# Dealing out weight conversions, and starting each group's first output tile one step sooner, in a fused gated-linear-attention and SoLU kernel

## The chip, the cores and the metric

The kernel runs on one core of one Trainium2 chip. The metric is the device time of one execution in microseconds, lower is better. A core has five engines, each with a queue of its own that it works through in order: TensorE (PE in the profile; its weight loads are shown apart as PEld), VectorE (DVE), ScalarE (ACT), GpSimd (POOL) and SyncE (SP), which here only issues transfers. Engines wait for each other by semaphores. TensorE writes to PSUM, which has eight banks.

## The reference

Two blocks are joined. The first is a gated linear recurrence over 768 tokens for 4 batches and 8 heads of width 48; the second multiplies by weights, applies a softmax-weighted activation and a layer norm, and multiplies by weights again (1024 hidden units).

```
for t in range(S):
    state = alpha[:, :, t, :, None] * state + einsum('bhd,bhe->bhde', k[:, :, t], v[:, :, t])
    y[:, :, t] = einsum('bhd,bhde->bhe', q[:, :, t], state)
x = y.transpose(0, 2, 1, 3).reshape(B * S, H * D)      # 3072 x 384
h = x @ w_in                                           # 3072 x 1024
e = exp(h - max(h));  solu = h * e / (sum(e) + 1e-9)
ln = (solu - mean(solu)) / sqrt(var(solu) + 1e-6) * g_ln
out = ln @ w_out                                       # 3072 x 384
```

q, k, v and alpha are float32. The three weight arrays come as float64 and have to be converted on the chip.

## The kernel before

The sequence is cut into six groups of 128 tokens per batch, 512 tokens in all. For every group the kernel computes attention (in a chunked form with scans for the decay), then the up product, the activation, and the down product. The whole order is written by hand: a manual schedule, in which the order of the code is the order on every engine's queue.

**The up part of a group.** `up(g, s)` runs for s = 0 to 7, one step for each 128 of the 1024 hidden units. TensorE makes h in PSUM (L394, one of two banks), ScalarE takes its exponential e (L408), VectorE makes u = h * e into `room` (L409), ScalarE squares u (L412). In the squares and exponentials lie the row sums for the norm, added up in `running` by POOL (e) and VectorE (u2) at L427. The norm is applied behind the down product as one factor for each row: `token_sums` (L454) gathers the sums on TensorE and VectorE once a group, and `finish` (L518) makes the factor on VectorE (L532 to L537) and POOL (a power, L546), scales on ScalarE (L548) and writes out.

**The down part.** A group has four tiles of 128 tokens (one for each batch), and the down product of a tile is eight matmuls, done in two halves of four (`down(n, half)`, L501). The tile's result lies in one of two PSUM banks until `finish` has read it. The halves of group g-1's four tiles are spread over the eight steps of group g, one in each step: `todo` (L909, L946) is the list of them. Group 0's downs stand in the prologue; so group 1 has none to do in its steps, and the last group's eight stand behind the loop.

**The attention of the next group.** Between the steps of group g the kernel does the attention of group g+1. Two plans, `usual` and `first` (L835 to L849), say at which step which piece is done, and whether at the head of the step, behind its up, in the middle or at its tail. `apart` (L243) and `keys_back` (L300) run on ScalarE, `queries` (L250) and `decay` (L255) on POOL, `scan_on`, `scan_back`, `masked` and the transposes on VectorE, `scores`, `read_state`, `read_values` and `next_state` on TensorE. `read_values` copies the result y to x on ScalarE (L363), which the next group's up reads. `scores` writes four banks (a0 to a3) that `keys_back`, the query transposes, y and others use in turn.

**The prologue.** The weights are fetched as eight pieces into slots of `room` (`fetch`, L567): pieces 0 to 3 are w_in, 4 to 7 are w_out. `bits(i)` (L603) converts a piece in five VectorE steps (L612, L615, L620, L623, L624). `in_range(i)` (L590) checks a piece in two ScalarE passes (L598, L601). `scaled(i)` multiplies a piece of w_out by the norm's gains (L631). Later pieces are fetched into slots whose earlier piece has been converted and checked. The eight steps of group 0 (L735) hold the conversions of pieces 2 to 5, two or three VectorE steps in each; pieces 6 and 7 are converted behind the loop (L759, L767). `alpha_over(g)` (L192) checks alpha in two ScalarE passes (L196); `load(alpha, an, g + 1)` may overwrite `an` only when it and `alpha_T(g)` (VectorE's transposes of alpha) have read it. `mean` (L638) sums w_out by column on TensorE, and `centre` (L655) adds the result to w_out on POOL in group 1, so that from group 1 on the mean of the norm needs no work of its own.

The loop of group 0 and the lines behind it, before the change:

```
    for f in range(FC):
        up_mm(0, f)
        if f == 4:
            array_sums(0, 0)
        up_act(0, f, (lambda: in_range(2 + f // 2, (f % 2,))) if f < 6 else None)
        bits(2 + f // 2, f % 2)
        ...
    bits(6)
    ...
    down(0, 0)
    scaled(6)
    bits(7)
    token_sums(0)
    alpha_T(1)
    down(1, 0)
```

Of the kernel before, what the change touches and what calls it, by code (L numbers as in the profile page):

```python
# [11 lines left out]
U32 = mybir.dt.uint32  # L12
I32 = mybir.dt.int32
AF = mybir.ActivationFunctionType
ALU = mybir.AluOpType
# [17 lines left out]
def fast_path(ctx, tc, q, k, v, alpha, moe_w_in, moe_w_out, moe_g_ln, out):  # L33
# [13 lines left out]
    B, H, S, D = q.shape  # L47
    NTOK, DM = out.shape
    DFF = moe_w_in.shape[1]
    G = S // P  # L50
# [136 lines left out]
    def alpha_T(g):  # L187
        nc.gpsimd.memset(aT[:, :, 0:1], 0.0)
        firsts(an, aT[:, 0:H, 1:SW])
        lasts(an, aT[:, H:NB, 1:SW])  # L190

    def alpha_over(g):  # L192
        x = an.rearrange("p h u d -> p (h u d)")
        sq = one.tile([P, 768], FP, name="sq").bitcast(U8)[:, 0 : x.shape[1]]
        for i, sign in enumerate((1.0, -1.0)):
            nc.scalar.activation(  # L196
                out=sq, in_=x, func=AF.Relu, scale=sign, bias=mone, accum_out=over[:, g, i : i + 1]
            )
# [201 lines left out]
    def up_act(g, f, between=None):  # L400
        d = gr[g]
        h = d["h"]
        if g:
            e, u2 = (ring.tile([P, T4], FP, name=x) for x in ("e", "u2"))
        else:
            e, u2 = (sT[:, f % 4, 4 * i : 4 * i + 4].rearrange("p b t -> p (b t)") for i in range(2))
        u = u_of(g, f)
        nc.scalar.activation(out=e, in_=h, func=AF.Exp)  # L408
        nc.vector.tensor_tensor(out=u, in0=h, in1=e, op=ALU.mult)  # L409
        if between:  # L410
            between()
        nc.scalar.activation(out=u2, in_=u, func=AF.Square)  # L412
        d[f] = e, u2
# [87 lines left out]
    def down(n, half, part=range(HF)):  # L501
        g, b = divmod(n, B)
        d = st[n]
        if half == 0 and 0 in part:
            d["o"] = ps_o.tile([P, 512], FP, tag="o", name="o")
        for f in (half * HF + i for i in part):
            nc.tensor.matmul(  # L507
                d["o"][:, 0 : DM + 1], lhsT=u_of(g, f)[:, b * P : b * P + P], rhs=w_out[:, f], start=(f == 0),
                stop=(f == FC - 1), skip_group_check=True,
            )  # L510
# [50 lines left out]
    def place(i):  # L561
        kind, f = pieces[i]
        return w_out[:, f : f + 2, 0:DM] if kind else w_in[:, :, f * P : f * P + 2 * P]
# [26 lines left out]
    def in_range(i, parts=(0, 1)):  # L590


        if not float64:
            return
        if 0 in parts:
            hi = raws[i][:, :, :, 1].bitcast(FP)
            squares[i] = one.tile([P, F], FP, name="sq").rearrange("p (c f) -> p c f", c=hi.shape[1])
            nc.scalar.activation(out=squares[i], in_=hi, func=AF.Square, accum_out=far[:, i, 0:1])  # L598
        if 1 in parts:
            sq = squares.pop(i)  # L600
            nc.scalar.activation(out=sq, in_=sq, func=AF.Exp, scale=-(2.0**24), accum_out=far[:, i, 1:2])  # L601

    def bits(i, part=None):  # L603
        if not float64:
            return
        lo, hi = raws[i][:, :, :, 0], raws[i][:, :, :, 1]
        if part != 1:
            made[i] = [
                lots[2 * (i % 2) + x].rearrange("p (c f) -> p c f", c=hi.shape[1]) for x in range(2)
            ]  # L610
            top = made[i][0].bitcast(U32)
            nc.vector.tensor_scalar(  # L612
                out=top, in0=hi, scalar1=3, scalar2=0x3FFFFFF8, op0=ALU.logical_shift_left, op1=ALU.bitwise_and
            )
            nc.vector.scalar_tensor_tensor(  # L615
                out=top, in0=hi, scalar=0xC0000000, in1=top, op0=ALU.bitwise_and, op1=ALU.bitwise_or
            )
        if part != 0:
            top, low = made.pop(i)
            nc.vector.tensor_scalar(  # L620
                out=low.bitcast(U32), in0=top.bitcast(U32), scalar1=0xFF800000, scalar2=None, op0=ALU.bitwise_and
            )
            nc.vector.scalar_tensor_tensor(out=low, in0=lo, scalar=2.0**-52, in1=low, op0=ALU.mult, op1=ALU.mult)  # L623
            nc.vector.tensor_tensor(out=place(i), in0=low, in1=top, op=ALU.add)  # L624

    def scaled(i):
# [103 lines left out]
    keys_back(0)  # L730
    in_range(0)
    bits(1)
    in_range(1)

    for f in range(FC):  # L735
        up_mm(0, f)
        if f == 4:
            array_sums(0, 0)
        up_act(0, f, (lambda: in_range(2 + f // 2, (f % 2,))) if f < 6 else None)

        bits(2 + f // 2, f % 2)
        if f == 0:
            next_state(0)
            fetch(4, 3)
            load_first(k, kn, 1)
            load_first(q, qn, 1)
            load(alpha, an, 1)
        elif f == 2:
            ends_k = ends_of(kn, "e")
        elif f == 3:  # L750
            fetch(5, 1)
            fetch(6, 2)
            ends_q = ends_of(qn, "u2")
        elif f == 5:
            fetch(7, 3)
            load_v(1)
        elif f == 6:
            scaled(4)
    bits(6)  # L759
    tk = three("tp_k", [(ps_a, "a2"), (ps_a, "a3"), (ps_h, "h")])  # L760
    turned(kn, ends_k, tk)
    load(k, kn, 2)
# [1 line left out]
    scaled(5)  # L764
    down(0, 0)
    scaled(6)
    bits(7)  # L767
    token_sums(0)
    alpha_T(1)
    down(1, 0)  # L770
    scaled(7)
    tq = three("tp_q", [(ps_a, "a0"), (ps_a, "a1")])
# [8 lines left out]
    mean(1)  # L781
    down(0, 1, (2, 3))
    hold(0)
    alpha_over(1)
    load(alpha, an, 2)
    tq += three("tp_q2", [(ps_h, "h")])
    turned(qn, ends_q, tq, range(H, NB))
    down(1, 1)
# [121 lines left out]
    for g in range(1, G + 1):  # L910
        rise, att = g < G, g + 1 < G
        plan = first if g == 1 else usual

        def at(where, s):
            for what in plan[where].get(s, "").split() if att else ():
                attend(g + 1, what)

        after = 3 if g == 1 else None
        if not rise:
            break  # L920
        for s in range(FC):
            at("head", s)
            if rise:
                up(g, s)
            if after is not None:
                finish(after)
                after = None
            if s == 0 and g < 3:
                next_state(g)
            if s == 0 and g > 1:  # L930
                token_sums(g - 1)
            at("behind", s)
            for f in centres.get(s, ()) if g == 1 else ():
                centre(f)
            if rise and s:
                running(g, s)
            at("middle", s)
            if todo:
                n, half = todo.pop(0)
                down(n, half)  # L940
                if half:
                    after = n
            at("tail", s)
        if after is not None:
            finish(after)
        todo = [(n, half) for n in range(g * B, g * B + B) for half in range(2)]  # L946


    for n, half in todo[:2]:
        down(n, half)  # L950
        if half == 0:
            token_sums(G - 1)
            last_norm()
    finish(G * B - B)
# [485 lines left out]
```

## Time and profile before

| what | value |
|---|---|
| time, median of 3 runs | 373.24 us (372.33 to 374.39) |
| the profiled execution's own time | 374.51 us |
| its span, first to last instruction | 372.6 us |
| mean granted TensorE clock | 0.995 |
| busy: TensorE / VectorE / ScalarE / POOL | 361.1 / 244.9 / 147.2 / 124.6 us |
| down products (L507), up products (L394) on TensorE | 134.8, 132.2 us busy |
| VectorE, the 40 conversion steps (L612, L615, L620, L623, L624) | 5.4 + 7.7 + 4.4 + 7.7 + 7.6 = 32.8 us busy |
| transfers | 36.06 MB, mean 97 GB/s |

How to read it: the profile shows one execution on the chip. A line names the kernel's line, the engine, the operation, and the tiles written and read; "[0.60 <-ACT x L363]" says that the engine stood idle for 0.60 us before the instruction and what ended that. TensorE's ends are modelled, so its busy time is no measure of how well it runs, but its idle time is idle. In a float32 product each matmul appears twice. A busy share is an average over stages with different limits; the stages here are the prologue (to about 100 us), the middle groups, and the last group with its tail.

### The profile page before, as it was taken

To read this page: it belongs to the slowest core of one execution; us is meant where nothing else is said; L and a number is where in the kernel's file an instruction comes from. 1 tells how busy PE (TensorE), PEld (TensorE's weight loads), DVE (VectorE), ACT (ScalarE), POOL (GpSimd) and SP (SyncE) were. 2 spreads that over 40 slices of the span, in tenths; PEclk is the share of its full clock that TensorE was granted. 3 is DMA by queue.
4 is the path that set the end of the run, shared out by engine and by line. 5 is a ranking of instruction groups with operands and counts; after the bars stand their busy time and mean duration, and the time that the engine had idled before them with its cause. 6 is when DMAs were issued, how large, how long until landed. Compare 5 with 4: busy or idle time off the path is not lost. (4 is left out here: it accounts for less than half of the span.)

```text
span 372.6 us, 10040 instructions
## 1 busy us (share of the span) xinstructions
PE 361.1 (97%) x4341; PEld 215.8 (58%) x4341; DVE 244.9 (66%) x375; ACT 147.2 (40%) x260; POOL 124.6 (33%) x129
## 2 busy tenths in 40 slices
PE   8889999979999999999999999999999999999994
PEld 7775355556755566566575566575555565555552
DVE  1997979978998888945666945666946223544500
ACT  3649853591556262251532251532231231332100
POOL 7020000001367973573114573114582211333200
PEclk9999999998999999999999999999999999999999
DMA  9995986066177608453036253004050000000011
GB/s 181 187 326 144 217 270 139 2 135 152 67 161 165 153 3 168 111 137 84 25 86 145 68 136 86 25 4 106 21 129 9 23 23 0 24 22 21 30 39 49
DMA packets 72871, 36.06 MB, mean 97 GB/s; under 512 B 48232, under 2 KB 70000, under 8 KB 72816
## 3 DMA queue, kind: packets, MB, share of 16 engines
q1 hardware_dynamic: 71792, 34.39, 39.5%
q10 hardware_dynamic: 1024, 0.92, 0.7%
q8 instruction: 36, 0.59, 0.7%
q14 instruction: 19, 0.16, 0.1%
HBM read 25.30 MB, written 4.72 MB: 81 GB/s over the span
## 5 line engine op out<-in xcount | busy, mean ns | idle before, releaser
L507 PE MATMUL o<-w_out,room 128*128 128x385 f32 x384 | 134.8, 495 | 0.0
L394 PE MATMUL h<-x,w_in 128*128 128x512 f32 x288 | 132.2, 599 | 0.6 <-ACT x L363 0.6
L507 PEld LDWEIGHTS o<-w_out,room 128*128 128x128 f32 x384 | 71.6, 191 | 55.3 <-issue 14.7
L394 PEld LDWEIGHTS h<-x,w_in 128*128 128x128 f32 x288 | 52.7, 189 | 58.3 <-issue 48.4
L409 DVE TENSOR_TENSOR room<-h,e 128x512 f32<-128x512 f32 x40 | 27.6, 690 | 60.0 <-ACT e L408 60.0
L408 ACT ACTIVATE e<-h 128x512 f32<-128x512 f32 x40 | 23.9, 597 | 93.8 <-PE h L394 93.6
L427 POOL TENSOR_TENSOR p<-p,e 128x512 f32<-128x512 f32 x30 | 42.5, 1416 | 27.3 <-ACT e L408 27.0
L412 ACT ACTIVATE u<-room 128x512 f32<-128x512 f32 x40 | 25.2, 630 | 38.2 <-DVE room L409 38.2
L546 POOL TENSOR_TENSOR r<-sums,mhalf 128x1 f32<-128x1 f32 x20 | 12.8, 639 | 77.3 <-DVE sums L537 77.1
L289 DVE TENSOR_TENSOR sT<-a,mask 128x512 f32<-128x512 f32 x43 | 26.7, 683 | 14.4 <-PE a L278 14.4
L427 DVE TENSOR_TENSOR p<-p,u 128x512 f32<-128x512 f32 x30 | 24.4, 814 | 7.2 <-ACT u L412 7.2
L204 DVE TENSOR_TENSOR_SCAN hT<-aT,unit 128x516 f32<-128x516 f32 x18 | 23.4, 1342 | 7.6 <-ACT aT L697 7.5
L204 DVE TENSOR_TENSOR_SCAN aT<-aT,seed 128x516 f32<-128x516 f32 x18 | 27.9, 1578 | 0.2
L278 PEld LDWEIGHTS a<-qv,kT 32*128 32x128 f32 x704 | 21.9, 189 | 8.8 <-DVE qv L799 2.7
L278 PE MATMUL a<-qv,kT 32*128 32x128 f32 x704 | 24.6, 282 | 2.1 <-DVE qv L799 1.9
L333 PE MATMUL y<-sT,vn 128*32 128x128 f32 x768 | 22.9, 274 | 1.0 <-issue 0.8
L212 POOL COPY fend<-hT 128x12 f32<-128x12 f32 x6 | 4.1, 676 | 59.0 <-DVE hT L204 59.0
L333 PEld LDWEIGHTS y<-sT,vn 128*32 128x32 f32 x768 | 20.8, 110 | 4.4 <-issue 3.8
L225 POOL TENSOR_TENSOR kT<-kT,hT 128x1024 f32<-128x1024 f32 (+1 forms) x8 | 14.2, 1805 | 21.1 <-DVE kT L179 21.1
L196 ACT ACTIVATE sq<-an,mone 128x1536 uint8<-128x1536 f32 x12 | 18.9, 1575 | 0.2
L548 ACT ACTIVATE o_sb<-o,r 128x384 f32<-128x384 f32 x16 | 9.3, 581 | 24.1 <-POOL r L546 24.1
L363 ACT COPY x<-y 128x384 f32<-128x384 f32 x24 | 11.2, 479 | 7.3 <-PE y L333 7.1
(148 smaller groups left out, 364.5 us busy)
## 6 DMA issues: line engine op xcount, KB each, us to landing
vn<-in_v_dram SPq DMA_DIRECT2D x24, 192.0 KB, 4.4
an<-in_alpha_dram SPq DMA_DIRECT2D x20, 192.0 KB, 4.2
out_dram<-o_sb SPq DMA_DIRECT2D x20, 192.0 KB, 1.9
room<-in_moe_w_out_dram SPq DMA_DIRECT2D x8, 384.0 KB, 4.8
kn<-in_k_dram SPq DMA_DIRECT2D x16, 192.0 KB, 4.2
qn<-in_q_dram SPq DMA_DIRECT2D x16, 192.0 KB, 3.9
lot<-qe SPq DMA_DIRECT2D x40, 64.5 KB, 2.1
lot<-qv SPq DMA_DIRECT2D x20, 129.0 KB, 2.4
```

What stands on the lines that cost most here:

```text
L196: nc.scalar.activation(out=sq, in_=x, func=AF.Relu, scale=sign, bias=mone, accum_out=over[:, g, i : i + 1])
L204: nc.vector.tensor_tensor_scan(out=o, data0=a, data1=s, initial=1.0, op0=ALU.mult, op1=ALU.add)
L225: nc.gpsimd.tensor_tensor(out=kT[:, part], in0=kT[:, part], in1=hk[:, part], op=ALU.mult)
L278: nc.tensor.matmul(a[b][:, i], lhsT=kT[quarter(b), kb], rhs=qv[quarter(b), qb, 0:P], start=not last and not i, stop=bool(last), tile_posit ...
L289: nc.vector.tensor_tensor(out=sT[:, b, half * NP : half * NP + NP], in0=a[b], in1=mask[:, None, :].to_broadcast([P, NP, P]), op=ALU.mult,)
L333: nc.tensor.matmul(y_bank(b)[quarter(r), a], lhsT=lhsT, rhs=rhs, start=(b, r) not in begun, stop=stop, tile_position=(row, 32 * r), skip_g ...
L394: nc.tensor.matmul(h, lhsT=w_in[:, a, f * P : (f + 1) * P], rhs=d["x"][:, a].rearrange("p b t -> p (b t)"), start=(a == 0), stop=(a == KC ...
L408: nc.scalar.activation(out=e, in_=h, func=AF.Exp)
L409: nc.vector.tensor_tensor(out=u, in0=h, in1=e, op=ALU.mult)
L412: nc.scalar.activation(out=u2, in_=u, func=AF.Square)
L427: eng.tensor_tensor(out=p, in0=d[0][i] if f == 1 else p, in1=d[f][i], op=ALU.add)
L507: nc.tensor.matmul(d["o"][:, 0 : DM + 1], lhsT=u_of(g, f)[:, b * P : b * P + P], rhs=w_out[:, f], start=(f == 0), stop=(f == FC - 1), skip ...
```

## The change

Four things are moved; no instruction is added or taken away.

1. The five steps of a conversion can be called one by one (`bit(i, k)`), and the 30 steps of pieces 2 to 7 are dealt out over the eight steps of group 0: 4, 2, 3, 3, 3, 3, 3 and 9 behind the u of each step, where 2 and 3 stood in turn and ten more behind the loop.
2. The check of piece 1 moves from ahead of group 0's loop into its step 4, and both halves of piece 4's check stand in step 5.
3. `alpha_over(1)` moves from behind `hold(0)` to where `bits(7)` stood, ahead of `token_sums(0)`, and `load(alpha, an, 2)` to just behind `alpha_T(1)`.
4. In groups 1 to 4 the first half of the group's own first tile is done in step 7 of that group, so that each of the later halves stands one step sooner and each `finish` at an odd step where it stood at an even one. Group 1, which had none, has one half in step 7; group 5 has none there, and in the tail its row sums stand behind both halves of its first tile, where they stood behind one.

```
-    in_range(1)
+    steps = [(i, step) for i in range(2, 8) for step in range(5)]
+    checks = {0: [(2, 0)], 1: [(2, 1)], 2: [(3, 0)], 3: [(3, 1)], 4: [(1, 0), (1, 1)], 5: [(4, 0), (4, 1)]}
+    def check(f):
+        for i, part in checks.get(f, ()):
+            in_range(i, (part,))
     for f in range(FC):
         up_mm(0, f)
...
-        up_act(0, f, (lambda: in_range(2 + f // 2, (f % 2,))) if f < 6 else None)
-        bits(2 + f // 2, f % 2)
+        up_act(0, f, lambda: check(f))
+        for _ in range((4, 2, 3, 3, 3, 3, 3, 9)[f]):
+            step = steps.pop(0)
+            if float64:
+                bit(*step)
...
-    bits(6)
...
     scaled(6)
-    bits(7)
+    alpha_over(1)
     token_sums(0)
     alpha_T(1)
+    load(alpha, an, 2)
     down(1, 0)
...
     hold(0)
-    alpha_over(1)
-    load(alpha, an, 2)
...
             at("middle", s)
+            if s == FC - 1 and g < G - 1:
+                todo.append((g * B, 0))
             if todo:
                 n, half = todo.pop(0)
                 down(n, half)
...
-        todo = [(n, half) for n in range(g * B, g * B + B) for half in range(2)]
+        todo = [(n, half) for n in range(g * B, g * B + B) for half in range(2)][g < G - 1 :]
     for n, half in todo[:2]:
         down(n, half)
-        if half == 0:
+        if half == 1:
             token_sums(G - 1)
             last_norm()
```

`bit(i, k)` holds the same five VectorE instructions that `bits` held, k choosing one of them.

## The prediction

> **What bounds the kernel now.** I read the busy tenths first. In the page's second part a slice is 9.3 us.
>
> ```profile
> PE   8889999979999999999999999999999999999994
> ...
> PEclk9999999998999999999999999999999999999999
> ```
>
> TensorE is full nearly everywhere, at full clock, except in slice 9 (74 to 84 us), where a clock digit falls too. So only what TensorE waits for can be won. Its waits, longest first:
>
> ```profile
> PE a L278 <- DVE qv L799: 1.9, 2, 1.4
> ...
> PE h L394 <- ACT x L363: 0.6, 1, 0.6
> PE sums L645 <- DVE cols L467: 0.6, 1, 0.6
> ```
>
> The other entries lie before 28 us, where nothing changes. The windows around the longest wait (columns: stretch, length, TensorE busy, granted clock, DMA):
>
> ```profile
> 79.00:79.77 0.77, 0.23 (x1) 1.00 1.11 224
> 79.77:81.60 1.83, 0.48 (x2) 1.00 0.76 140
> 81.60:82.95 1.35, 1.31 (x44) 1.00 0.46 107
> 82.95:86.36 3.41, 3.41 (x30) 0.50 0.55 122
> 86.36:90.00 3.64, 3.64 (x70) 1.00 0.92 213
> ```
>
> TensorE stands nearly idle for 2 us, and 1.3 us later its clock is halved for 3.41 us, which therefore hold only 1.7 us of full-speed work. The wait with its price is thus about 2.2 + 1.7 us. Who is late is in the timeline of VectorE:
>
> ```profile
> 34.27 0.69 DVE L409 TENSOR_TENSOR room<-h,sT 128x512 f32<-128x512 f32 x1 [1.88 <-ACT sT L408]
> ...
> 48.87 0.69 DVE L409 TENSOR_TENSOR room<-h,sT 128x512 f32<-128x512 f32 x1 [1.22 <-ACT sT L408]
> ...
> 54.81 0.69 DVE L409 TENSOR_TENSOR room<-h,sT 128x512 f32<-128x512 f32 x1 [0.74 <-ACT sT L408]
> ...
> 80.89 0.69 DVE L799 TENSOR_TENSOR qv<-tp_q,aT 128x512 f32<-128x512 f32 x1
> 83.91 0.69 DVE L289 TENSOR_TENSOR sT<-a,mask 128x512 f32<-128x512 f32 x1 [2.33 <-PE a L278]
> ```
>
> From 54.81 to 81.58 VectorE works without a gap: 13 conversion steps (to 66.05), row sums, alpha's transposes, six scans, keys, queries. Before that it idles 1.88 + 1.22 + 0.74 us, waiting for ScalarE's exponentials. The fault is order, not load. From 144 us on TensorE has no wait over 0.25 us.
>
> **Conversions dealt out.** A piece costs 0.55 + 0.96 + 0.55 + 0.96 + 0.96 us, with gaps 4.1. Before, 17 of 30 steps precede the last u (L409, 54.81) and 13 follow; after, 21 and 9. Does it fit? The first exponential ran at 33.66 because the check of piece 1 (31.72 to 33.66) stood before it; that check goes to step 4, so u starts at about 32.4, when the second conversion ends. From 32.4 to 54.81 are 22.4 us; 21 steps (17.1) and seven u's of 0.61 (4.3) are 21.4. Adding row by row, each u waiting for its exponential, I get the last u at 54.95, 0.14 late. The four steps that are gone from behind it ran from 55.41 to 58.47: 3.06 us. Net: the chain to the last qv is 2.9 us shorter, and that qv is ready at 78.7.
>
> The check moved into step 4 takes 1.9 us of ScalarE where it idled 1.33 us; piece 4's whole check then sits in step 5, and the exponential of step 6 starts about 0.3 us later (51.1 for 50.81); its u waited for VectorE until 51.93, which hides it. Transfers: piece 5 can be fetched from 42.8 (step 3 of piece 3 ends at 42.3, SP is busy until 42.82) and is needed at 49.6; the room loads took 3.5 to 8.6 us to land, median 5.2. So between 0 and 1.8 us of VectorE time; I take 0, by the median. Piece 7 goes out near 49.7 and is needed at 59.
>
> **Alpha's check and load sooner.** Two ScalarE passes with their reads, 71.94 to 75.36: 3.4 us. They now stand between the scalings of pieces 6 and 7. Piece 6 is converted at about 59.1, scaled by 60.5; the check ends at 63.9; the last conversion ends at 63.1, so the last scaling is 0.8 us late and done at 65.0. Behind it on ScalarE waits the mean's copy; TensorE comes to the mean's sums only at 65.8. Cost nothing; without that cover up to 0.8. The four loads of alpha leave SP at 67 and not from 75.34 to 77.13. SP issued the query moves behind them at 77.92; those now need qe at 75.0, and SP is free. Value nothing by itself: VectorE took alpha at 86.31 after the masks, not after the load.
>
> **What TensorE gains.** The 0.6 at the mean's sums goes, but the next wait swallows it: TensorE comes to the first scores of group 1 at about 78.4 and waits until 78.75, where it started at 81.64. That is 2.9. The remaining idle stretch is under 0.5 us, so I take the halved clock as gone: 1.7 more, with ends 0 and 1.7. At the second half of the scores TensorE is 4.6 sooner. VectorE is not: between the two masks stands alpha's transposition, now from 83.0 to 86.0, so the second mask, which began at 90.13, begins at about 85.95: 4.2. From there VectorE hardly stops, and POOL's queries and TensorE hang on it:
>
> ```profile
> 117.72 1.45 PEld L278 LDWEIGHTS a<-qv,kT 32*128 32x128 f32 x46 [0.88 <-POOL qv L253]
> ```
>
> So at the next scores 4.2 us remain, 0.4 given back.
>
> The Trainium skill, "TensorE: Matmul & The Clock Gate", section "HAM oscillation — how this bites in real kernels", says that idle gaps up to about 3.4 us leave the clock up. By that rule the halving has another cause and would remain, and the sum below would be 1.7 us less. This trace halves it after gaps of 0.54 and 1.38 us; I go by the trace.
>
> **Downs one step sooner.** The halves of a group stay eight; no work goes. At the end of group 1 TensorE waits for the copy of the last y:
>
> ```profile
> 136.95 2.84 PE L394 MATMUL h<-x,w_in 128*128 128x512 f32 x6 [0.60 <-ACT x L363]
> ```
>
> Now a down half of 2.6 us stands there: gain 0.6. It needs w_out's first four chunks centred by POOL; the fourth is done at 130.64 against 136.3. If POOL were late by more than 5.7 us the cover would be gone.
>
> The finishes move from even to odd steps, and this is the risk. At step 3 of groups 2 to 4 ScalarE must now scale a row block before it splits the queries (L245) and copies the keys (L305, L310). The scale waits for POOL's power (0.55), which now stands behind the queries' products and a running sum:
>
> ```profile
> 160.88 1.72 POOL L427 TENSOR_TENSOR p<-p,e 128x512 f32<-128x512 f32 x1
> ```
>
> and in ScalarE's timeline there are
>
> ```profile
> 160.08 1.32 ACT L245 ACTIVATE qv<-qe,parity 128x512 f32<-128x512 f32 x2
> 161.31 1.05 ACT L305 COPY kg<-tp 128x512 f32<-128x512 f32 x2
> 162.25 0.66 ACT L310 COPY kg<-tp 128x256 f32<-128x256 f32 x2
> ```
>
> Sum for group 2: 162.60 + 0.55 + 0.05 + 0.58 = 163.8; queries and keys, 2.82 from first to last, end at 166.6. TensorE's scores began at 166.62 and need the banks that the keys leave. Step 4's exponential waits behind them too, 2.4 us later than its 164.13; its bank is wanted only two steps on. The margin is nil, and in group 3 (running sum done at 218.53, scores at 222.53) the same; group 4 has no keys to copy. Bounds 0 to 0.5 each (POOL's running sums took between 1.27 and 1.79); I take 0.1 each, as the sums meet almost exactly. At step 5 the state's decay on POOL goes behind a power, from 167.9 to about 173.4, and is read at 178.75: nothing. At step 7 the scale comes ahead of the copies of y, up to 0.9 late; the next h follows down and state products 4 us later: nothing.
>
> **Last group.** The row sums stay as far behind the last h as before (two down halves). The power then has two whole halves, 5.2 us, before a bank is wanted; it and the first finish took from 348.9 to 352.9. Nothing.
>
> **The sum.** 4.2 + 0.6 - 0.2 = 4.6 us, of which 1.7 is clock. Against the profiled execution, 374.51 - 4.6 = 369.9 (its span 372.6; 1.9 around it stays). The median of the runs, 373.24, is 1.27 lower; had it the same halving, it would come to 368.6. I cannot tell which part of the 1.27 belongs to the profile and which to the halving, so I forecast between the two: 369.3.
>
> **Rivals.**
> - *The usual execution has no halved clock.* For: the three runs spread over 2.06 us, about the price of one halving, and the profiled one is at the top. Against: nothing shows the clock of the others. Then 373.24 - (4.6 - 1.7) = 370.3. Chance 0.2.
> - *VectorE does not get its 2.9*: pieces land late or the exponentials do not keep up (1.8 of the 2.9 lost). Then TensorE still idles about 1.5 us and gains 1.1 + 0.6 - 0.2, the clock being open: 370.0 to 371.7. Against: 1 us of slack in the row-by-row sum. Chance 0.1.
> - *Nothing much changes*: VectorE's later chain at 90 to 117 us takes back more than 0.4. Against: only alpha's transposition binds it there. 371.5 to 373.5; chance 0.06.
> - *Slower*: POOL's power at step 3 is late by 2 us in groups 2 and 3, because sums and products there share time with VectorE's scans; TensorE idles 2 us at each of the two scores and, as at 79 us, loses 1.7 us of clock each time: 7.4 against 4.6, so 376. It decides from about 1 us of delay, where idle time alone still leaves the kernel faster. For: margin nil. Against: the same POOL work ends at the same place in both groups within 0.1 us. Chance 0.05.
>
> The forecast has 0.59. Range 367.8 to 371.6: the low end is 368.6 with 0.2 given to the scores at 166 not waiting and 0.6 more of spread; the high end takes in the first two rivals. A measurement of this kernel tells about 0.5% (1.9 us) from no change: faster by more 0.82, within 0.13, slower 0.05.
>
> **What would show it.** Right: VectorE's idle before L409 at 34 and 49 us gone; last qv near 78.7; TensorE's idle before the scores under 0.6 us; no window with clock 0.50; no wait at x L363. Wrong: half clock still there; a gap before the scores in groups 2 and 3 with ScalarE's keys behind POOL's r; last u (L409) of group 0 after 55.5.

## The result, and the profile after

The changed kernel takes 368.81 us (median of 4 runs, 368.56 to 369.21); the kernel before, run beside it, 373.55 us (4 runs, 372.33 to 374.39). The ratio is 0.9873, with a 95% interval of 0.9844 to 0.9901. The profiled execution took 369.21 us with a span of 367.4 us, where the one of before had taken 374.51 and 372.6. The prediction's range held the time and its forecast, 369.3, was 0.5 us too high.

The busy tenths of the page, in slices of 9.2 us:

```profile
PE   8999999999999999999999999999999999999994
...
PEclk9999999999999999999999999999999999999999
```

Slice 9 is full now, and no clock digit falls. TensorE's waits from 28 us on (line waited for, us in total, times, longest):

```profile
PE h L394 <- DVE g_col L642: 0.5, 1, 0.5
PE a L278 <- POOL qv L253: 0.3, 1, 0.3
```

The waits on the query products (1.9), on x (0.6) and on the mean's columns (0.6) are gone. The 0.5 stands at 28 us, in front of the moved work, and comes and goes between executions. The windows over the first and second scores of group 1 (stretch, length, TensorE busy, weight loads, VectorE, ScalarE, POOL, granted clock, DMA share, GB/s):

```profile
77.60:78.39 0.79, 0.79 (x3) 0.19 (x2) 0.76 (x2) 0.79 (x2) 0.00 (x0) 1.00 0.37 87
78.39:80.74 2.35, 2.35 (x65) 2.16 (x64) 0.39 (x2) 2.29 (x6) 0.00 (x0) 1.00 0.48 114
80.74:83.50 2.76, 2.76 (x11) 1.44 (x8) 2.76 (x5) 2.66 (x6) 0.00 (x0) 1.00 0.78 171
83.50:86.36 2.86, 2.86 (x68) 2.44 (x68) 2.86 (x3) 0.24 (x2) 1.71 (x3) 1.00 0.93 215
```

TensorE is busy in all of them, at full clock. VectorE's timeline (start, length, line, tiles, idle time before and what ended it) shows why, first the u's of group 0 (L409), then the last query product (now L811):

```profile
32.86 0.68 DVE L409 TENSOR_TENSOR room<-h,sT 128x512 f32<-128x512 f32 x1
...
49.01 0.69 DVE L409 TENSOR_TENSOR room<-h,sT 128x512 f32<-128x512 f32 x1 [0.50 <-ACT sT L408]
51.88 0.69 DVE L409 TENSOR_TENSOR room<-h,sT 128x512 f32<-128x512 f32 x1
54.81 0.68 DVE L409 TENSOR_TENSOR room<-h,sT 128x512 f32<-128x512 f32 x1
```

```profile
78.01 0.69 DVE L811 TENSOR_TENSOR qv<-tp_q,aT 128x512 f32<-128x512 f32 x1
80.66 2.48 DVE L289 TENSOR_TENSOR sT<-a,mask 128x512 f32<-128x512 f32 x4 [1.97 <-PE a L278]
83.06 2.04 DVE L179 STREAM_TRANSPOSE aT<-an 128x1024 f32<-128x1024 f32 x1
84.93 1.11 DVE L182 STREAM_TRANSPOSE aT<-an 128x512 f32<-128x512 f32 x1
85.86 2.49 DVE L289 TENSOR_TENSOR sT<-a,mask 128x512 f32<-128x512 f32 x4
```

Of the 1.88 + 1.22 + 0.74 us that VectorE stood idle ahead of u's, 0.50 is left. The last u comes at the same time as before with four conversion steps more done, and the last query product ends at 78.70 where it ended at 81.58. The second mask (85.86) now stands straight behind alpha's transposes; before, it waited for TensorE's scores:

```profile
90.13 2.48 DVE L289 TENSOR_TENSOR sT<-a,mask 128x512 f32<-128x512 f32 x4 [0.86 <-PE a L278]
```

At the next scores and at the end of group 1, TensorE's timeline reads

```profile
113.37 1.38 PE L278 MATMUL a<-qv,kT 32*128 32x128 f32 x36 [0.30 <-POOL qv L253]
```

```profile
131.84 2.86 PE L507 MATMUL o<-w_out,room 128*128 128x385 f32 x8
134.54 2.74 PE L394 MATMUL h<-x,w_in 128*128 128x512 f32 x6
```

that is 4.35 us sooner at the scores of group 2 (117.72 before). The h of group 2 starts without a wait, 2.41 us sooner although a down half of 2.70 us has been put ahead of it: 5.1 us in all. From there the lead stays at 5.1 to 5.2.

### The profile page after: what moved, and what is told of

The parts are those of the page before. It is cut to its first block, busy times and chain, and to the rows that moved or that the text cites. A ratio compares the mean times of both kernels' runs of the same rounds, so it can differ in the third digit from the quotient of the medians.

```text
span 367.4 us, 10036 instructions
## 1 busy us (share of the span) xinstructions
PE 359.7 (98%) x4341; PEld 215.9 (59%) x4341; DVE 245.4 (67%) x375; ACT 146.1 (40%) x260; POOL 131.1 (36%) x129
## 5 line engine op out<-in xcount | busy, mean ns | idle before, releaser
L409 DVE TENSOR_TENSOR room<-h,e 128x512 f32<-128x512 f32 x40 | 27.5, 688 | 73.7 <-ACT e L408 73.7
L546 POOL TENSOR_TENSOR r<-sums,mhalf 128x1 f32<-128x1 f32 x20 | 14.8, 739 | 72.9 <-DVE sums L537 72.7
L427 DVE TENSOR_TENSOR p<-p,u 128x512 f32<-128x512 f32 x30 | 23.1, 768 | 5.1 <-ACT u L412 5.1
L212 POOL COPY fend<-hT 128x12 f32<-128x12 f32 x6 | 3.0, 507 | 56.1 <-DVE hT L204 56.1
L261 POOL TENSOR_TENSOR state<-state,lot 128x384 f32<-128x384 f32 x10 | 8.8, 900 | 12.0 <-DMA lot<-qv 11.8
```

The lines of the kernel that those rows point to most:

```text
L427: eng.tensor_tensor(out=p, in0=d[0][i] if f == 1 else p, in1=d[f][i], op=ALU.add)
L546: nc.gpsimd.tensor_tensor(out=r, in0=s[:, 3:4], in1=mhalf, op=ALU.pow)
```

## The experiments

Each time is a median with its lowest and highest run; each ratio is against the kernel before on the same chip, with its 95% interval. In the edits "before" and "changed" name the kernel that was edited; "deal", "checks", "alpha" and "downs" are the four parts of the change in their order.

| run | what it is | us | ratio |
|---|---|---|---|
| e1_no_downs | changed, downs undone | 369.81 (369.38 to 370.09) | 0.9890 [0.9867, 0.9913] |
| e2_downs_only | before, with the downs | 371.82 (371.53 to 374.24) | 0.9943 [0.9923, 0.9963] |
| e3_warm_gap | before, 11 idle products in the gap | 375.03 (374.20 to 377.36) | 1.0052 [1.0028, 1.0077] |
| e4_conv_only | before, with deal and checks | 370.34 (370.16 to 371.19) | 0.9909 [0.9885, 0.9932] |
| e5_check_only | before, with the checks moved | 373.61 (372.85 to 374.48) | 0.9992 [0.9973, 1.0011] |
| e6_deal_only | before, with the deal | 371.37 (370.44 to 372.46) | 0.9939 [0.9915, 0.9962] |
| e7_alpha_only | before, with alpha sooner | 373.75 (372.40 to 375.66) | 0.9997 [0.9975, 1.0020] |
| e11_warm_wide | before, 3 wide idle products in the gap | 373.16 (373.02 to 373.67) | 0.9984 [0.9963, 1.0004] |
| e8_qv_late | changed, last query product 2.1 us late | 372.57 (370.97 to 375.63) | 0.9972 [0.9945, 0.9999] |
| e9_pool_late | changed, POOL late at step 3 | 372.33 (372.19 to 372.56) | 0.9951 [0.9932, 0.9971] |
| e10_split_alpha | changed, alpha_T(2) divided | 368.76 (368.43 to 369.48) | 0.9851 [0.9826, 0.9875] |
| e12_changed_again | changed, as it is | 369.01 (368.59 to 371.17) | 0.9886 [0.9855, 0.9916] |

The kernel before ran 73 times beside these. In 33 executions the mean granted clock was 0.995 or less, with a median of 374.40 us; in the other 40, the full-clock executions, it was 0.996 or more, with 373.06 us. The profiled execution of before (0.995) is of the first kind. One window of 3.41 us at half clock makes a mean of 0.995 over 372.6 us. So by this split the halved clock costs 1.35 us, and before has it in somewhat under half of its executions. The ten runs of the changed kernel (two measurements) lie at 0.996 to 1.0.

### What each part is worth

**e1_no_downs** takes the downs out of the changed kernel:

```
-            if s == FC - 1 and g < G - 1:
-                todo.append((g * B, 0))
...
-        todo = [(n, half) for n in range(g * B, g * B + B) for half in range(2)][g < G - 1 :]
+        todo = [(n, half) for n in range(g * B, g * B + B) for half in range(2)]
...
-        if half == 1:
+        if half == 0:
             token_sums(G - 1)
```

> The changed kernel with its fourth part undone: groups 1 to 5 take their down halves and finishes where the kernel before had them. My theory: the conversions carry 4.2 us, the earlier downs 0.6 (0.6 to 0.75, the idle ahead of the first up of group 2), so this stands at 369.5 us, 0.7 above the changed kernel's 368.8, and TensorE's idle of 0.60 us for the copy to x (L363) is back. Rival: moving the finishes to odd steps frees VectorE and POOL elsewhere, and the part is worth more than 1 us (370 us or more). Rival: the part is worth nothing, 368.8.

Measured 369.81, and the wait for x at the h of group 2 is back:

```profile
132.02 2.84 PE L394 MATMUL h<-x,w_in 128*128 128x512 f32 x6 [0.60 <-ACT x L363]
```

**e2_downs_only** is the reverse edit on the kernel before.

> The kernel before with the fourth part alone. My theory: 0.6 to 0.75 us less than before (about 372.9 of 373.5), the wait of TensorE on x (L363) gone, the wait on the last qv and the stretch with clock 0.50 as before. Rival: with the first half of the group's tile in step 7 and no conversions moved, POOL comes late with centring in group 1 and the gain is gone: 373.5.

Seven of its eight executions have the full clock and a median of 371.79, against 372.74 for the full-clock executions of before on that chip: 0.95 us. The eighth (374.24), which is the profiled one, has the halved clock, and a wait that is new: 0.7 us of TensorE for the state's decay. POOL's timeline shows what the decay stood for:

```profile
126.32 2.09 POOL L261 TENSOR_TENSOR state<-state,lot 128x384 f32<-128x384 f32 x2 [1.35 <-DMA lot<-qv]
```

The decay waits until the query rows have been moved, and a move that leaves a microsecond late (before, the same line waited 0.25) is paid on TensorE. SP's issues fit this: one of the four moves of these rows took 1.77 us to issue, where the others took 0.56 to 0.59, and two more stood behind it; in the profiled executions of before and of the changed kernel the long one (1.53 and 1.43 us) was the last. This wait of 0.6 or 0.7 us is also in the profiled executions of e7_alpha_only and e10_split_alpha, and not in the one of the changed kernel. By the traces the downs are worth 0.7 us: e1 reaches the h of group 2 at 132.02, the changed kernel at 131.84 (134.54 less the added half's 2.70) in spite of a prologue that ran 0.54 later. By the medians they are worth 0.8 to 1.0. 0.6 of it is the wait for x, and the rest has no line of its own.

**e4_conv_only** has the deal and the moved checks, with alpha and the downs as before; **e5_check_only** the moved checks alone:

```
-    in_range(1)
+    checks = {0: [(2, 0)], 1: [(2, 1)], 2: [(3, 0)], 3: [(3, 1)], 4: [(1, 0), (1, 1)], 5: [(4, 0), (4, 1)]}
...
-        up_act(0, f, (lambda: in_range(2 + f // 2, (f % 2,))) if f < 6 else None)
+        up_act(0, f, lambda: check(f))
```

**e6_deal_only** has the deal alone, with the check of piece 1 left where it was.

> The kernel before with the conversions dealt out and the check of piece 1 moved, alpha's check and load at their old place, downs as before. My theory: alpha's part is worth nothing by itself, so the same as the run with only the downs undone, 369.5 us, last qv near 78.7 us, clock 1.00. Rival: alpha's old place on ScalarE and SP comes into the way now that VectorE is 2.9 us sooner (the queries' moves wait behind alpha's load on SP, the keys' copies behind alpha's check on ScalarE): 0.5 to 1 us more, 370 to 370.5.

> The kernel before with only the checks of pieces 1 and 4 moved to steps 4 and 5; the old conversions, alpha and downs stay. Theory (the length of VectorE's conversions sets the last query product, and the earlier first u only moves idle time): the first u comes about 1.4 us sooner (32.9 in place of 34.27), VectorE waits that long again at a later step for ScalarE's exponential, the last u stays near 54.9 and the last query product near 81.6; time as before, that is runs near 372.7 with the full clock and near 374.2 where it is halved. Rival (the freed first exponential is itself the gain): 1.0 to 1.4 us less, 371.3 to 372.8.

> The kernel before with only the conversions dealt out as in the changed kernel; piece 1's check stays at its old place ahead of the first u, alpha and the downs as before. Theory: the first u stays at 34.3, so the dealt conversions fit one step later and VectorE's chain ends about 0.9 us later than with the check moved too; time about 371.3 (370.34 was measured with both). Rival A (the check's move is idle): 370.3. Rival B (the deal needs the freed first step; without it TensorE waits at several steps): 372.5 or more.

Together they bring 3.6 us (370.34 against 373.97; 2.4 against the full-clock executions alone, 372.74). The checks alone bring nothing: in VectorE's timeline of e5 the u's read

```profile
32.53 0.68 DVE L409 TENSOR_TENSOR room<-h,sT 128x512 f32<-128x512 f32 x1
36.32 0.69 DVE L409 TENSOR_TENSOR room<-h,sT 128x512 f32<-128x512 f32 x1 [1.25 <-ACT sT L408]
...
48.67 0.69 DVE L409 TENSOR_TENSOR room<-h,sT 128x512 f32<-128x512 f32 x1 [1.50 <-ACT sT L408]
...
54.61 0.69 DVE L409 TENSOR_TENSOR room<-h,sT 128x512 f32<-128x512 f32 x1 [0.73 <-ACT sT L408]
```

The first u is 1.74 us sooner, and VectorE waits 1.25 us at the second instead, and 1.50 in place of 1.22 at the sixth; the last one comes where it came. With the deal alone (e6) it is the other way round: the first u waits its 1.88 us, the last comes at 55.48, and TensorE pays once at a bank of h, in its timeline:

```profile
39.16 1.12 PE L394 MATMUL h<-x,w_in 128*128 128x512 f32 x2 [0.65 <-DVE room L409]
```

e6 is 1.03 us behind e4 by the medians (0.9 in the theory); they come from two chips, and against the full-clock executions of before on each (372.74 and 373.07) it is 0.7. The moved check gains nothing without work to put into the freed time; the deal alone gains 2.2 of the 3.6 us, or 1.7 of the 2.4 against full-clock executions.

e4's 370.34 is 0.8 above the theory's 369.5. Its profiled execution has a wait which the changed kernel's does not show, of VectorE at the first conversion step of piece 5:

```profile
DVE lot L616 <- DMA room<-in_moe_w_out_dram: 0.5, 1, 0.5
```

The dealt conversions come to piece 5 at 49.6 us. In the changed kernel's profiled execution its two transfers had landed at 47.48 and 48.46; in e8 they left SP a microsecond later and landed at 49.26 and 50.25, for a wait of 0.9, and in e12 VectorE waited 0.75. In three of the eight profiled executions with the new deal VectorE comes too early for piece 5.

**e7_alpha_only** moves only alpha's check and load.

> The kernel before with only alpha's check ahead of the bits of piece 7 and alpha's load behind alpha_T(1). Theory: the last query product is what ends last, and it stays near 81.6, so the time is that of before: 372.7 with the full clock, 374.2 with the halved one. Rival (its old place costs by itself, as the 0.5 us between the two runs with the new conversions suggest): 0.4 to 0.6 us less, both ways.

373.75, nothing. Yet e4, which lacks alpha's part, is 0.53 us behind e1, which has it. Of this, 0.37 us follows the wait for piece 5, which is chance: e4's second half of the scores of group 1 starts that much later. Another 0.3 to 0.4 comes at 90 us, where the second reading of the state by the queries takes 1.45 us in e4 and 1.16 in e1. SP issued the moves of the query rows at 75.94 behind alpha's four loads in e4, and at 74.49 in e1, where alpha had gone out sooner; that this made the reading longer is not shown, as the profile names no wait there. Nor does it last: at the scores of group 2 e1 waits 0.35 us for POOL's queries and e4 not at all, and the two are 0.34 us apart again (112.88 and 113.22). A later loss of e4, 0.4 us at the row sums near 137 us, has no cause on record. So no gain of alpha's part is shown, alone or beside the conversions.

### What the late query product and the clock cost

**e3_warm_gap** fills TensorE's gap of before, so that its clock should not fall and nothing else is sooner:

```
     down(2, 0)
+    warm(11, ps_h, "h")
     scores(1, 0)
```

> The kernel before with 11 products of ones by ones (a result that nothing reads) between the third tile's first down half and the first scores of group 1, so that TensorE works where it stood idle and the scores still start when the last qv is there. It tells the clock's price from the idle's. My theory: the halved clock comes from the idle time and is gone (clock 1.00 all through); 1.7 us are won at the scores, of which VectorE, with alpha's transposition between the masks, lets 1.1 through: 372.4 us. Rival (gaps under 3.4 us do not count and the halving has another cause): clock 0.50 near 83 us still there, 373.5 us.

In the profiled execution the clock stayed full, and the scores of group 2 came 1.73 us sooner than in the profiled execution of before (115.99 against 117.72). The time did not: 375.03. Four of the ten executions have a mean clock of 0.992 to 0.995 and take 376.39 to 377.36; where it fell in them is not on record. The other six have a median of 374.5, still 1.8 us above the full-clock executions of before on that chip (372.74). In TensorE's timeline of the profiled one, which is one of the six, 1.3 us are lost later, in the middle of a group's row sums:

```profile
139.49 0.65 PE L462 MATMUL rows<-p,ones 128*32 128x64 f32 x30
141.41 0.30 PE L462 MATMUL rows<-p,ones 128*32 128x64 f32 x2 [1.27 <-issue]
```

"issue" means that no wait in the profile explains the pause: 30 of 32 equal products have run, and two are left. I suspected the supply of instructions. One queue of the page's third part is of the kind instruction, with 36 packets and 0.59 MB, so 16 KB each, and the 11 added products move every later instruction along in these blocks. (The Trainium skill, "Runtime: NRT & Kernel Launch", section "Instruction fetch mechanics", has blocks of this size and calls the cost of crossing their boundary mostly hidden; if a block made this pause, it was not hidden here.) **e11_warm_wide** fills the same gap with three wide products and takes three idle ones away at the start, so that each later instruction keeps its place:

```
-    warm(14)
+    warm(11)
...
     down(2, 0)
+    x = ps_h.tile([P, 512], FP, tag="h", name="warm")
+    for _ in range(3):
+        nc.tensor.matmul(x, lhsT=ones, rhs=u_of(0, 0), start=True, stop=True)
     scores(1, 0)
```

> The kernel before with 3 idle products of 512 columns ahead of the scores of group 1 (1.29 us of TensorE's idle time, as the 11 idle products of 128 columns had filled), and 3 fewer idle products at the very start, so that every later instruction of TensorE keeps its place in the program. Theory (the halved clock costs 1.4 to 2.0 us, and the run with 11 products lost this to a pause of 1.3 us in the row sums that no wait explains, because 11 more instructions shifted where TensorE's program blocks are fetched): no pause at the row sums, no halved clock, all runs at 372.0 to 372.8, none near 374.2. Rival (idle products ahead of the scores cost time by themselves): 374.2 to 375.2, as with 11.

The pause is gone, and all ten executions lie within 373.02 to 373.67: none near 374.4. Their 373.16 is that of the full-clock executions of before on the same chip (373.07), as it should be if the halving is all that separates the two groups. The expected 372.0 to 372.8 was too low: by the medians, nothing is sooner in this kernel than in a full-clock execution of before. That the place of the instructions made e3's pause is possible after this pair, and is not shown: e11 also has fewer and wider products, and the runs do not tell why a block would be late.

**e8_qv_late** makes the last query product late again in the changed kernel, by three repeats of the product ahead of it:

```
-    nc.vector.tensor_tensor(out=qe[:, :, 0:P], in0=tq[2], in1=aT[:, H:NB, 1:SW], op=ALU.mult)
+    for _ in range(4):
+        nc.vector.tensor_tensor(out=qe[:, :, 0:P], in0=tq[2], in1=aT[:, H:NB, 1:SW], op=ALU.mult)
```

> The changed kernel with the query product of the ends (0.69 us on VectorE) made four times in place of once, so that everything behind it on VectorE, the last two query products among it, comes 2.1 us later. Theory (this chain sets the scores of group 1): the last query product is ready at 80.8 in place of 78.7; 2.1 us more, 370.9, where the clock stays full, and 372.2 to 372.6 where TensorE's gap halves it, so two groups of runs. Rival (the chain is hidden by now, and the gain came from elsewhere): 368.8 to 369.4.

Three of ten executions have a clock of 0.997 or more and take 370.97 to 371.78, 2.2 to 3.0 us above the changed kernel, as expected; the other seven have 0.995 or less and take 372.31 to 375.63, with a median of 373.57 where 372.2 to 372.6 was expected. Some of their mean clocks, down to 0.988, are lower than one halved window makes, and their traces are not on record. Lateness at this place is paid in full, and the halved clock comes back with it.

When the clock falls can be read from these traces. In the profiled executions of before, e2 and e5 it falls 78.51 us after it first rose, in e7 after 75.09; that is 23 and 22 times 3.413 us, and each time it stays down for 3.41. So the clock is decided on a grid of 3.41 us. Here are the windows of that grid ahead of the halving, in before and in e7, and then two windows of e8's profiled execution, whose clock stayed up (third column: TensorE busy; the 1.00 or 0.50 behind POOL's column is the clock):

```profile
76.12:79.53 3.41, 3.11 (x13) 1.68 (x11) 3.27 (x4) 2.95 (x7) 0.00 (x0) 1.00 0.96 213
79.53:82.94 3.41, 1.79 (x46) 1.60 (x50) 2.02 (x3) 3.31 (x8) 0.00 (x0) 1.00 0.67 131
82.94:86.36 3.42, 3.42 (x30) 2.28 (x25) 2.45 (x5) 2.05 (x6) 0.00 (x0) 0.50 0.55 122
```

```profile
78.15:81.56 3.41, 1.82 (x7) 0.74 (x5) 3.34 (x4) 3.35 (x7) 0.00 (x0) 1.00 0.30 72
81.56:84.97 3.41, 3.31 (x59) 3.32 (x62) 0.04 (x1) 3.31 (x8) 0.00 (x0) 0.50 0.38 88
```

```profile
76.63:80.04 3.41, 2.12 (x8) 0.90 (x6) 3.34 (x5) 2.37 (x5) 0.00 (x0) 1.00 0.14 34
80.04:83.46 3.42, 2.07 (x63) 1.95 (x63) 1.42 (x3) 3.33 (x7) 0.00 (x0) 1.00 0.44 104
83.46:86.87 3.41, 3.41 (x32) 2.06 (x36) 3.41 (x5) 1.32 (x4) 0.00 (x0) 1.00 0.61 131
```

After a window with 1.59 us of TensorE idle (3.41 less 1.82) or 1.62 the clock is halved for the next one; after 1.29 or 1.35 it is not, although e8 idles more in sum. In all 14 profiled executions, up to TensorE's last products, no window ahead of a full-clock one has more than 1.35, and each of the four halvings follows one with 1.59 to 1.84. So it is the idle time inside one window that counts (as the profile counts it, with modelled ends of TensorE's products), and whether a gap falls into one window or is divided by a boundary depends on when the clock first rose, which was between 3.9 and 7.2 us after the start of the span in the 14. Before's two gaps are 0.54 and 1.38 us, 2.4 us from the first's start to the second's end. A grid laid at random has 1.59 us of them in one window for 1.66 of its 3.41 us, about half of the time (an estimate from these rows); 33 of 73 were counted.

The Trainium skill, "TensorE: Matmul & The Clock Gate", section "What's actually happening", has the clock follow a free-running window of 3413 ns. The traces agree on the window. The rule of the page that the prediction weighed, idle gaps up to about 3.4 us being harmless, does not hold here: two gaps, the longer of 1.38 us, were enough.

### The margin at step 3

**e9_pool_late** tests the risk that the prediction named, with two idle sums on POOL ahead of the power at step 3 of groups 2 and 3:

```
+            if g in (2, 3) and s == 3:
+                for _ in range(2):
+                    x = lot[:, 2064:2576]
+                    nc.gpsimd.tensor_tensor(out=x, in0=x, in1=x, op=ALU.add)
             if after is not None:
                 finish(after)
```

> The changed kernel with two idle sums of 128x512 on POOL (1.27 us each by the row of the running sums) ahead of the finish at step 3 of groups 2 and 3. Theory: the sums push the power that ScalarE waits for, the margin of the trace ahead of the scores there (0.57 us in group 2, 0.37 in group 3) is used up and the rest is paid: 2.0 and 2.2 us, 372.9 to 373.2 in all, and up to 1.5 us more for each gap that halves the clock. Rival (ScalarE has other work and the finish is slack by several us): 368.8, no change.

First the changed kernel without them, group 2, in the timelines of POOL, ScalarE and TensorE:

```profile
157.72 1.79 POOL L427 TENSOR_TENSOR p<-p,e 128x512 f32<-128x512 f32 x1
159.47 0.55 POOL L546 TENSOR_TENSOR r<-sums,mhalf 128x1 f32<-128x1 f32 x1
```

```profile
160.04 0.58 ACT L548 ACTIVATE o_sb<-o,r 128x384 f32<-128x384 f32 x1 [3.02 <-POOL r L546]
160.52 1.33 ACT L245 ACTIVATE qv<-qe,parity 128x512 f32<-128x512 f32 x2
161.75 1.05 ACT L305 COPY kg<-tp 128x512 f32<-128x512 f32 x2
162.69 0.66 ACT L310 COPY kg<-tp 128x256 f32<-128x256 f32 x2
```

```profile
163.93 2.07 PE L278 MATMUL a<-qv,kT 32*128 32x128 f32 x64
```

The power does stand behind the running sum, and ScalarE does wait for it, as predicted; but the keys' last copies end at 163.36 and the scores begin at 163.93 without a wait. The margin is 0.57 us, in group 3 0.37 (219.49 and 219.86). And e9, with the power late, ScalarE behind it, and TensorE in both groups:

```profile
161.40 0.55 POOL L546 TENSOR_TENSOR r<-sums,mhalf 128x1 f32<-128x1 f32 x1
```

```profile
161.98 0.58 ACT L548 ACTIVATE o_sb<-o,r 128x384 f32<-128x384 f32 x1 [5.14 <-POOL r L546]
```

```profile
164.40 2.78 PE L278 MATMUL a<-qv,kT 32*128 32x128 f32 x60 [0.57 <-ACT kg L305]
```

```profile
222.13 2.12 PE L278 MATMUL a<-qv,kT 32*128 32x128 f32 x36 [0.78 <-ACT kg L305]
```

e9's execution began 0.18 us sooner, so the scale was 2.12 us late. By the margins that leaves 2.12 - 0.57 = 1.55 and 2.12 - 0.37 = 1.75 to pay; TensorE's later starts moved by 1.60 in group 2 and by 1.78 in group 3. Their sum, 3.4, is close to the measured 372.33 less 368.81, 3.5. (The two sums took 2.11 us from start to start, not the 2.54 that the expectation had.) The clock stayed full: 0.85 us is the most idle time that the profile counts in one window. The rest of the delay lies in scores that ran longer, 2.99 us for 2.07 in group 2, which counts as busy.

### A version beyond the change

**e10_split_alpha** divides the transposition that stands ahead of the second mask:

```
+    lasts(an, aT[:, H:NB, 1:SW])
     masked(0)
-    alpha_T(2)
+    nc.gpsimd.memset(aT[:, :, 0:1], 0.0)
+    firsts(an, aT[:, 0:H, 1:SW])
```

> The changed kernel with alpha_T(2) divided: its last rows' part stays ahead of the first mask, its memset and first rows' part go behind both masks' first one. Theory: the second mask, which stands behind alpha_T(2) on VectorE, comes about 0.4 us sooner (85.4 in place of 85.86) and the rest of the wait at the scores of group 2 goes: 0.3 to 0.4 us less, 368.4 to 368.5. Rival (the wait at the scores of group 2 is POOL's own, behind the queries, and stays): 368.8, within 0.1.

> The changed kernel once more, to set the version with alpha_T(2) divided against it by one yardstick: the runs of the kernel before with the full clock (its other runs, 1.4 us longer, left out). By that yardstick the divided version stands at 368.76 against 373.33, 0.988. If dividing gains the 0.3 to 0.4 us expected of it, the changed kernel stands at 0.9885 to 0.989 here; if the wait at the scores of group 2 is worth nothing, at 0.988 or below.

In VectorE's timeline of e10 a pause is now between the transposition and the second mask:

```profile
82.76 2.02 DVE L179 STREAM_TRANSPOSE aT<-an 128x1024 f32<-128x1024 f32 x1
85.31 2.48 DVE L289 TENSOR_TENSOR sT<-a,mask 128x512 f32<-128x512 f32 x4 [0.53 <-PE a L278]
```

The mask waits for the scores, so VectorE is no longer what binds there. Corrected for a start 0.3 us sooner, it comes 0.25 sooner, and the scores of group 2 come 0.2 sooner. The profiled execution then loses 0.6 to the state's decay, for the moved rows that e2 showed. Against the full-clock executions of before, e10 stands at 0.9878 (368.76 to 373.33) and the changed kernel, run again, at 0.9891 (369.01 to 373.08): 0.5 us. Both sets of runs overlap and came from two chips, so a gain of 0.2 to 0.5 us is likely and not settled.

## Why the prediction was right, step by step

- **Conversions dealt out: right.** Last u 54.81 (predicted 54.95), last query product ready at 78.70 (78.7). Alone (e4) it brings 3.6 of the 4.7 us by the medians, and 2.4 of 4.1 where both kernels have the full clock. The transfers were taken at 0 with bounds of 0 to 1.8; they cost 0 in five of eight profiled executions and 0.5 to 0.9 in three.
- **Alpha's check and load, nothing by itself: right** as the only edit (e7, 0.9997). Beside the conversions no lasting gain is shown either: e1 is 0.53 us ahead of e4, but what the traces tie to a cause there is the wait for piece 5.
- **What TensorE gains: right in mechanism, 0.15 us small.** 4.35 us at the scores of group 2 for a predicted 4.2; the second mask at 85.86 for 85.95. That alpha's transposes give 0.4 back was right: in e10, with a part of them moved away, VectorE waits there.
- **The clock: right in the main point, mis-sized.** It goes with the gap, as the prediction held against the page's rule. Taken at 1.7 us, it costs 1.35 over 73 executions, and before has it in 45% of them.
- **Downs: right.** 0.6 predicted, 0.7 in the traces, 0.8 to 1.0 in the medians. The last group was taken at nothing; from the last scores to the end the changed kernel is 0.1 us longer than e1.
- **The step that failed: "The margin is nil ... I take 0.1 each".** The two terms are 0. The sum put the power behind a running sum as the old trace timed it, against the scores of the old trace. But the running sum moved from 160.88 to 157.72 and the scores from 166.62 to 163.93: from one to the other are 6.21 us where there were 5.74, and this 0.47 us is most of the margin. It goes with the downs: 5.80 us in e1, which lacks them, and 6.23 in e2, which has them alone. VectorE's timelines of before and of the changed kernel show where it comes from:

```profile
153.98 0.68 DVE L409 TENSOR_TENSOR room<-h,e 128x512 f32<-128x512 f32 x1
...
154.95 0.16 DVE L537 TENSOR_TENSOR sums<-t,s 128x1 f32<-128x1 f32 x1
155.33 1.17 DVE L182 STREAM_TRANSPOSE qe<-qn 128x512 f32<-128x512 f32 x1 [0.21 <-issue]
```

```profile
151.66 0.68 DVE L409 TENSOR_TENSOR room<-h,e 128x512 f32<-128x512 f32 x1
152.26 1.12 DVE L182 STREAM_TRANSPOSE qe<-qn 128x512 f32<-128x512 f32 x1
```

Before, step 2's finish (L532 to L537) stood on VectorE between the u and the transposition of the queries. Moved to an odd step it leaves that place, and the transposition starts 0.60 us after the u and not 1.35. POOL's products, and the running sum behind them, hang on it: POOL waits 1.67 us for it (0.55 before). What a moved piece of work leaves behind was not counted on the engine that it left.

- **The sum.** 4.6 predicted between profiled executions, 5.3 measured (374.51 to 369.21): 0.15 at the scores of group 2, 0.15 more by the h of group 2, 0.2 at step 3 that was not lost, and 0.2 in smaller pieces. That the forecast came within 0.5 us is in part luck: it stood halfway between two starting points, 0.6 us below the sum from the profiled execution, and that covered most of the 0.7 by which the sum was short.
- **The first rival** (no halved clock in the usual execution, 370.3) has its condition in 40 of 73 executions, but its price was wrong. It took the whole 1.7 off the sum, though 0.4 of the clock's gain had been given back in the sum already, the halving is worth 1.35, and the other terms were 0.5 short. Full clock against full clock the change gains about 4.1 us (373.06 against 368.81 to 369.01), and against a halved one 5.4 to 5.6 (374.40). The 4.7 between the medians is the mixture.
- **The slower rival** priced its mechanism properly: e9 makes POOL 2 us late and TensorE's later starts move by 1.6 and 1.8 us. Its addition of two halved clocks did not come; the profile counts at most 0.85 us of idle time in a window there.

## What to carry to other kernels

Look for idle time of a loaded engine early in a long chain, and give it work that the chain does later anyway; freeing the engine's first wait alone (e5) moved the idle time and not the end. When a step is moved, re-time the engines that it leaves as well as the ones it joins, since the new margin is set by both. When the runs of one kernel fall into two groups, compare like with like, by the granted clock of each run, before a gain of one per cent is divided among causes.

## What the runs showed of the hardware that was not expected

- The clock is decided on a grid of 3.413 us counted from its first rise, by the idle time inside one window: 1.59 us and more halved the next window, 1.35 and less did not, in 14 profiled executions, and nothing in between was measured.
- Where that grid lies differs from execution to execution (the first rise at 3.9 to 7.2 us). This fits the two groups of times, 1.35 us apart, that one kernel shows with nothing changed.
- Eleven idle products of 128 columns in TensorE's gap left the kernel 1.8 us above the full-clock executions of before on the same chip, even with the full clock (374.5 against 372.74), and three of 512 columns that filled the same time 0.1 us (373.16 against 373.07). 1.27 us of it is a pause some 59 us later, in products that have nothing to do with them; its cause is open.
